# Loading the first K in front of the query weights in a decode step of attention and a gated feed-forward layer

## The chip, the cores and the metric

The kernel runs on one core of a Trainium2 chip. The metric is the device time of one execution in microseconds; lower is better. A core has TensorE for matmuls (PE in the profile; its loads of stationary operands are PEld), VectorE (DVE), ScalarE (ACT), GpSimd (POOL) and SyncE (SP), each with its own instruction stream. They meet through semaphores only. A DMA is issued by one of these streams and carried out by 16 DMA engines that all streams share. On-chip memory is SBUF, with 128 partitions; matmuls write to PSUM.

## What is computed

One token for each of 4 sequences goes through an attention block with a cache and then a gated feed-forward block, each behind a layer norm and with a residual. Cut to what matters:

```python
B, Sq, D = 4, 1, 512
H, Sk, Dh = 32, 8192, 128            # k_cache, v_cache: (B, H, Sk, Dh), bf16

def _A_ref(x, k_cache, v_cache, wq, wo):
    q = (x @ wq).reshape(B, Sq, H, Dh).transpose(0, 2, 1, 3)
    scores = jnp.einsum("bhqd,bhkd->bhqk", q, k_cache) * (Dh ** -0.5)
    p = _softmax(scores, axis=-1)
    o = jnp.einsum("bhqk,bhkd->bhqd", p, v_cache)
    return o.transpose(0, 2, 1, 3).reshape(B, Sq, H * Dh) @ wo

h  = x + _A_ref(_layernorm(x), k_cache, v_cache, wq, wo)
h2 = h + _B_ref(_layernorm(h), w_gate, w_up, w_down)   # (sigmoid(h@w_gate) * (h@w_up)) @ w_down
```

The two caches are 268 MB each, all other inputs together about 13 MB. Every byte is used once.

## The kernel before

The cache is worked through in 32 units (`NU`), each of 4 heads of one sequence. A unit's K is 128 partitions x 64 KB (8.4 MB), and its V likewise. SBUF holds three such places in the tile KV: K of even units in slot 0, K of odd units in slot 1, every V but the last in slot 2. The query weights wq (128 partitions x 32 KB, 4.2 MB) use slot 2 too, ahead of the first V. The names K0, K1, V0 and so on stand for the unit's number below.

At the start, the input x is loaded from ScalarE's queue, normalised and transposed (lines 272 to 292). Then TensorE multiplies it with wq (L301, in two halves of 16 matmuls, waiting for the semaphore of wq), VectorE transposes the result (L308, twice), gathers it in `q_all` (L309), and for each unit lays the query of that unit out as a stationary operand, Lq (`q_window`, L328).

A unit then runs as follows. `scores`: for 16 chunks of K, VectorE transposes a chunk (`k_chunk`, L335) and TensorE multiplies it with the query (four matmuls, L344). There are two places for transposed chunks, so from the third chunk on VectorE waits for TensorE's product with the chunk two before. `maxima`: after the last transpose VectorE writes one word (L361), whose semaphore says that this unit's K is no longer needed; it then finds the maxima (L362 to L367), and ScalarE takes the exponential (L369). In between, `pv` multiplies the weights of the unit before with its V (L405), ScalarE copies the result out (L410), and TensorE gathers it (L415); the first of those gathering matmuls says that this V is no longer needed. `weights` transposes the exponentials (L375). Every stream takes its instructions in the order written, so VectorE comes to L335 of unit 0 only after L308, L309 and L328.

All of the big loads are issued by SP, in one list:

```python
order = [("k", 0)] + [x for u in range(1, NU) for x in (("k", u), ("v", u - 1))] + [("v", NU - 1)]
for n, (x, u) in enumerate(order):
    w = t_qp if n == 2 else None
    if n >= 3:
        w = t_kd[u - 2] if x == "k" else t_kd[NU - 2] if u == NU - 1 else t_vd[u - 1]
```

So wq goes first, then K0 and K1 with no wait, then V0, which waits for the query's matmuls (`t_qp`, since it overwrites wq), then K2, which waits for the transposes of K0 (`t_kd[0]`), V1, which waits for the product with V0 (`t_vd[0]`), K3, which waits for the transposes of K1, and so on in pairs of a V and a K. SP takes them in order: a K whose slot is free still waits behind a V whose slot is not. At the end SP loads wo, w_gate and w_up into slot 1 and w_down into slot 2 (L546 to L557). The final matmuls with w_down (L521), two copies (L529, L530) and the store (L559) follow.

Of the kernel before, what the change touches and what calls it, by code (L numbers as in the profile page):

```python
# [18 lines left out]
class _Prog:  # L19
# [52 lines left out]
    def emit(self, eng, fn, waits=(), incs=1, ch=None):  # L72
        todo = self._waits(eng, waits)
        key = ch or eng
        tok = self.token(key, incs) if incs else None
        self._put(eng, todo, key, fn, incs, 1)
        return tok
# [41 lines left out]
def bass_sequential_preLN__mha_block_cached__glu_gated_glu__decode_kernel(  # L119
# [13 lines left out]
    _, H, S, DH = A_k_cache.shape  # L133
    F = B_w_gate.shape[1]
    assert DH == 128 and H == 32 and D == 512 and F % 128 == 0 and B == 4 and S == 8192
    NC = D // 128
# [17 lines left out]
    prog = _Prog({"p2d": "dve", "d2d": "dve", "a2d": "dve", "d2p": "pe", "a2p": "pe",  # L154
                  "d2a": "act", "p2a": "act",
                  "k0": "dve", "k1": "dve", "v2": "pe"})
    emit = prog.emit

    with ExitStack() as es:
# [40 lines left out]
        def reg(slot, off, size):  # L200
            return KV[:, slot * SLOT + off:slot * SLOT + off + size]
# [26 lines left out]
        t_wq = prog.token("wq", 16)  # L228
# [296 lines left out]
        for t in range(NFT):  # L525
            if t == 0:
# [2 lines left out]
        t_o = [emit("dve", lambda e: e.tensor_copy(o_sb[:, 0:HD], bank[DN][0:B, 0:HD]), [t_d]),  # L529
               emit("act", lambda e: e.activation(o_sb[:, HD:D], bank[DN][32:32 + B, 0:HD], ACT.Copy), [t_d])]  # L530

        prog.dma("sp", "wq", lambda e: e.dma_start(reg(2, 0, NC * H * DH), A_wq.rearrange("(p c) f -> p (c f)", p=128)),
                 tok=t_wq)
        for n, (x, u) in enumerate(order):
            w = t_qp if n == 2 else None
            if n >= 3:
                w = t_kd[u - 2] if x == "k" else t_kd[NU - 2] if u == NU - 1 else t_vd[u - 1]
            slot = slots[x, u]
            cache = A_v_cache if x == "v" else A_k_cache
            src = cache[u // (NU // B), HU * (u % (NU // B)):HU * (u % (NU // B) + 1), :, :].rearrange("h (p r) d -> (h p) (r d)", p=32)  # L540
            prog.dma("sp", f"{x}{slot}", lambda e, src=src, slot=slot: e.dma_start(reg(slot, 0, SLOT), src), [w],  # L541
                     tok=toks[x, u])
        for _ in range(40):
            emit("sp", lambda e: e.nop(), ch="pad")
        k_done, v_done = t_kd[NU - 1], t_vd[NU - 2]
# [46 lines left out]
```

## Time and profile before

| what | value |
|---|---|
| median of 3 runs | 1276.89 us (1276.79 to 1276.95) |
| span of the profiled execution | 1275.6 us |
| PE, DVE, ACT, POOL busy | 779.7, 762.3, 59.0, 5.7 us |
| read from HBM | 550.77 MB |
| transposes of K, L335 | 512, 1232 ns each |
| score matmuls, L344 | 2048, 420 ns each |

The profiled execution's own time is its span and what lies around it, 1.3 us less than the median by the two rows of the table. In the profile a row of an engine's timeline gives the start, the duration, the engine, the line and the operation, then the count if several are merged, and in brackets how long the engine was idle ahead of it and what ended that. "SPq" and "ACTq" are issues of DMAs. In the rows by stretches of time the columns are the length of the stretch, then for PE, PEld, DVE, ACT and POOL the busy time and the number of instructions, then the granted TensorE clock (1.00 is full speed), the summed busy share of the 16 DMA engines and the rate in GB/s.

### The profile page before, as it was taken

How to read it: one execution, taken by the hardware profiler on the slowest of the kernel's cores; microseconds unless marked ns; L12 is line 12 of the kernel's file. 1: busy time of each engine (PE TensorE's matmuls, PEld its weight loads, DVE VectorE, ACT ScalarE, POOL GpSimd, SP SyncE). 2: the span in 40 equal slices, each digit the busy share in tenths (PEclk: the TensorE clock that was granted, in tenths of full speed). 3: DMA queues.
4: the chain of work that ended last, by engine and by line, in shares of the span. 5: the costliest groups of instructions: out<-in, count | busy, mean ns of one | idle time of the engine just before them, and what ended most of it. 6: DMA issues, size and time to landing. Idle time of an engine off the chain costs nothing.

```text
span 1275.6 us, 14073 instructions
## 1 busy us (share of the span) xinstructions
PE 779.7 (61%) x4588; PEld 328.5 (26%) x4636; DVE 762.3 (60%) x917; ACT 59.0 (5%) x114; POOL 5.7 (0%) x22
## 2 busy tenths in 40 slices
PE   1676755557755557655567655567555577555577
PEld 0232222223222223222222222222222232222233
DVE  1876665556665557665567655566655566655571
ACT  2000000000000000000000000000000000000001
POOL 1000000000000000000000000000000000000000
PEclk8888877788877788877788777788777888777888
DMA  9999999999999999999999999999999999999998
GB/s 423 432 426 430 427 450 434 430 430 427 454 430 430 430 427 454 432 427 430 430 452 432 427 430 434 450 430 427 430 440 444 430 427 430 442 442 430 430 427 371
DMA packets 10244, 550.83 MB, mean 432 GB/s; under 512 B 1144, under 2 KB 1152, under 8 KB 1408
## 3 DMA queue, kind: packets, MB, share of 16 engines
q1 hardware_dynamic: 10224, 550.77, 99.7%
q8 instruction: 2, 0.03, 0.0%
q10 hardware_dynamic: 16, 0.01, 0.0%
q14 instruction: 2, 0.02, 0.0%
HBM read 550.77 MB, written 0.00 MB: 432 GB/s over the span
## 4 chain that ended last, share of the span: by engine, by line
DMA 60%; PE 20%; DVE 12%; issue 2%; ACT 1%; SPq 0%; DVEq 0%
DMA KV<-in_A_k_cache_dram 58%; PE PS L344 14%; DVE kT L335 12%; PE PS L405 5%; DMA KV<-in_B_w_down_dram 3%; ACT kT L410 1%; PE PS L415 0%; SPq L541 0%; DVE PTz L375 0%; PE PS L521 0%; DVE KV L529 0%; SPq L557 0%; DVEq L112 0%
## 5 line engine op out<-in xcount | busy, mean ns | idle before, releaser
L344 PE MATMUL PS<-kT,Lq 128*128 128x512 bf16 x2048 | 588.7, 420 | 343.5 <-DVE kT L335 326.4
L335 DVE STREAM_TRANSPOSE kT<-KV 128x1024 f32<-128x1024 f32 x512 | 614.4, 1232 | 300.3 <-DMA KV<-in_A_k_cache_dram 237.5
L344 PEld LDWEIGHTS PS<-kT,Lq 128*128 x2048 | 210.3, 103 | 694.6 <-issue 621.7
L375 DVE STREAM_TRANSPOSE PTz<-E_sb 32x512 bf16<-32x512 bf16 x128 | 89.9, 703 | 129.1 <-PE PS L415 125.5
L405 PE MATMUL PS<-KV,PTz 128*16 128x512 bf16 x2048 | 117.0, 381 | 0.0
L379 PE MATMUL PS<-part,headw 128*128 128x2 f32 x64 | 18.8, 363 | 100.4 <-DVE PTz L375 100.4
L369 ACT ACTIVATE E_sb<-PS,negm 128x512 bf16<-128x512 f32 x32 | 22.0, 687 | 1139.4 <-DVE negm L367 1139.4
L405 PEld LDWEIGHTS PS<-KV,PTz 128*16 128x16 bf16 x2048 | 58.9, 111 | 56.3 <-issue 13.6
L415 PE MATMUL PS<-lane,kT 128*128 128x4 f32 x256 | 33.6, 255 | 31.0 <-ACT kT L410 31.0
L362 DVE TENSOR_REDUCE part<-PS 128x1 f32<-128x512 f32 x32 | 22.1, 691 | 38.7 <-PE PS L344 38.7
L415 PEld LDWEIGHTS PS<-lane,kT 128*128 128x128 f32 x256 | 31.0, 191 | 46.2 <-issue 44.8
L379 PEld LDWEIGHTS PS<-part,headw 128*128 128x128 f32 x64 | 16.0, 310 | 103.7 <-DVE PTz L375 103.7
L410 ACT ACTIVATE kT<-PS,rsb 128x512 f32<-128x512 f32 x32 | 22.0, 687 | 61.5 <-PE PS L405 61.5
L388 PE MATMUL PS<-Lq 128*128 128x512 bf16 x27 | 11.0, 462 | 2.9 <-issue 2.5
L328 DVE TENSOR_TENSOR Lq<-q_all,mask 128x32 bf16<-128x32 bf16 x32 | 9.5, 297 | 0.0
L454 DVE TENSOR_TENSOR kT<-PS,mask 128x512 bf16<-128x512 f32 x1 | 0.7, 692 | 13.3 <-PE PS L415 13.3
L367 DVE STREAM_TRANSPOSE negm<-mxr 128x32 f32<-128x32 f32 x32 | 6.8, 212 | 1.1
L364 DVE STREAM_TRANSPOSE turn<-part 128x32 f32<-128x32 f32 x32 | 6.8, 211 | 1.1
L388 PEld LDWEIGHTS PS<-Lq 128*128 128x128 bf16 x44 | 4.8, 116 | 8.3 <-issue 6.1
L322 PEld LDWEIGHTS PS<-Lq,headw 128*128 128x128 bf16 x32 | 3.5, 108 | 12.8 <-issue 11.3
L396 DVE RECIPROCAL rsb<-PS 128x1 f32<-128x1 f32 x32 | 6.3, 197 | 0.7 <-PE PS L379 0.7
L301 PE MATMUL PS<-KV,kT 128*4 128x512 bf16 x32 | 3.6, 627 | 5.0 <-DMA KV<-in_A_wq_dram 5.0
(70 smaller groups left out, 56.7 us busy)
## 6 DMA issues: line engine op xcount, KB each, us to landing
KV<-in_A_wq_dram SPq DMA_DIRECT2D x1, 4096.0 KB, 12.2
KV<-in_A_wo_dram SPq DMA_DIRECT2D x1, 4096.0 KB, 27.2
KV<-in_B_w_gate_dram SPq DMA_DIRECT2D x1, 1792.0 KB, 31.1
KV<-in_B_w_up_dram SPq DMA_DIRECT2D x1, 1792.0 KB, 34.9
KV<-in_B_w_down_dram SPq DMA_DIRECT2D x1, 1024.0 KB, 32.1
KV<-in_A_k_cache_dram SPq DMA_DIRECT2D x32, 49.6
KV<-in_A_v_cache_dram SPq DMA_DIRECT2D x32, 30.7
KV<-in_B_w_down_dram SPq DMA_DIRECT2D x1, 512.0 KB, 32.9
```

The lines of the kernel that those rows point to most:

```text
L328: t_lq[u] = emit("dve", lambda e, ix: e.tensor_tensor(dst, bass.AP(raw(q_all), at(ix, 0) * (4 * TU) + 4 * (u - TU * t), [[NU * 4, 128], [1 ...
L335: t_tr[u, c] = emit("dve", lambda e: e.transpose(kT[:, (c % 2) * TW:(c % 2 + 1) * TW], KVw[:, o:o + TW]), w, ch="d2p")
L344: ins = e.matmul(bank[SBK], bass.AP(raw(Lq), ix[-1] * 2 + (128 * t + c % 2), [[528, 128], [1, 128]]), rhs, start=False, stop=False, skip_g ...
L362: a = emit("dve", lambda e: e.tensor_reduce(part[:, 0:1], bank[SBK], AX.X, ALU.max), [t_sc[u, NT - 1], t_pool], ch="d2d")
L364: a = emit("dve", lambda e: e.transpose(turn_[:, :], part[:, :]), [a], ch="d2d")
L369: t_exp[u] = emit("act", lambda e: e.activation(E_sb[:, :], bank[SBK], ACT.Exp, bias=negm[:, 0:1], scale=SCALE, accum_out=part[:, 1:2]), [ ...
L375: return [e.transpose(PTz[32 * q:32 * (q + 1), :].rearrange("p (r q c) -> p r q c", r=4, q=4)[:, :, q, :], E_sb[32 * q:32 * (q + 1), :].re ...
L379: t_sum[u] = emit("pe", lambda e: e.matmul(bank[QB[1]][:, 0:2], headw[:, :], part[:, 0:2], start=True, stop=True), [t_ptz[u], t_selc], ch= ...
L388: emit("pe", lambda e: [e.matmul(bank[XS], Lq[:, 0:128], Lq[:, 0:512], start=True, stop=True) for _ in range(n)][-1], [t_ps0, t_lq[NU - 1] ...
L405: made.append(e.matmul(PS[32 * j:32 * j + 16, ob:ob + 512], lhsT, KV[:, slot * SLOT + 512 * k:slot * SLOT + 512 * (k + 1)], start=(k < 4), ...
L410: t_ocp[u] = emit("act", lambda e: e.activation(O_sb, bank[OBK], ACT.Copy, scale=rsb[:, 0:1]), [t_pv[u], t_rs[u]], ch="a2p")
L415: ins = e.matmul(bass.AP(raw(PS), at(ix, 0) * 4 + (512 * EX + 4 * (u - t)), [[4096, 128], [1, 4]]), O_sb[:, 128 * q:128 * (q + 1)], lane[: ...
```

## The change

The load of wq becomes a function, `load_wq`, and is called in the loop behind the first entry of the list. So SP issues K0, wq, K1, and then the rest as before. The waits, the semaphores, the slots and every instruction of the other engines stay as they are; lines behind the edit get a number higher by up to four (the issues of K and V, L541 before, are L543 after).

```diff
-        prog.dma("sp", "wq", lambda e: e.dma_start(reg(2, 0, NC * H * DH), A_wq.rearrange("(p c) f -> p (c f)", p=128)),
-                 tok=t_wq)
+        def load_wq():
+            prog.dma("sp", "wq", lambda e: e.dma_start(reg(2, 0, NC * H * DH), A_wq.rearrange("(p c) f -> p (c f)", p=128)),
+                     tok=t_wq)
+
         for n, (x, u) in enumerate(order):
...
             prog.dma("sp", f"{x}{slot}", lambda e, src=src, slot=slot: e.dma_start(reg(slot, 0, SLOT), src), [w],
                      tok=toks[x, u])
+            if n == 0:
+                load_wq()
```

SP's list at its start, before (the tile KV is named for all of the loads; `s_pe` is the wait of V0 for the query's matmuls, `s_d2x` that of K2 for the transposes of K0, `s_p2x` that of V1 for the product with V0):

```order
L532 DMA KV<-in_A_wq_dram 128x16384 [waits barrier_Pool_Activation_PE_DVE_SP_release]
L541 DMA KV<-in_A_k_cache_dram 128x32768 x2
L541 DMA KV<-in_A_v_cache_dram 128x32768 [waits s_pe]
L541 DMA KV<-in_A_k_cache_dram 128x32768 [waits s_d2x]
L541 DMA KV<-in_A_v_cache_dram 128x32768 [waits s_p2x]
```

The same place of SP's list after the change:

```order
L543 DMA KV<-in_A_k_cache_dram 128x32768 [waits barrier_Pool_Activation_PE_DVE_SP_release]
L533 DMA KV<-in_A_wq_dram 128x16384
L543 DMA KV<-in_A_k_cache_dram 128x32768
L543 DMA KV<-in_A_v_cache_dram 128x32768 [waits s_pe]
L543 DMA KV<-in_A_k_cache_dram 128x32768 [waits s_d2x]
L543 DMA KV<-in_A_v_cache_dram 128x32768 [waits s_p2x]
```

Only the first two entries have changed places. VectorE's list from the query to the end of unit 0's transposes stands after the change as it stood before (`s_k0` is the wait for K0, `s_p2d` that for TensorE's product with an earlier chunk):

```order
L308 STREAM_TRANSPOSE kT<-PS 128x2x8x32 [waits s_pe] x2
L309 CAST q_all<-kT 128x8x4x4 [waits s_dve]
L328 TENSOR_TENSOR Lq<-q_all,mask 128x32 [waits s_pool,s_dve]
L335 STREAM_TRANSPOSE kT<-KV 128x1024 [waits s_k0]
L335 STREAM_TRANSPOSE kT<-KV 128x1024
L335 STREAM_TRANSPOSE kT<-KV 128x1024 [waits s_p2d] x14
L361 MEMSET dumm 128x1
```

Nothing has moved here: the transposes of K0 stand behind the three steps of the query.

## The prediction

> **What bounds the kernel now.** I read the page first: its span, its traffic and the chain that ended last.
>
> ```profile
> span 1275.6 us, 14073 instructions
> ...
> HBM read 550.77 MB, written 0.00 MB: 432 GB/s over the span
> ...
> DMA 60%; PE 20%; DVE 12%; issue 2%; ACT 1%; SPq 0%; DVEq 0%
> ```
>
> The bytes come at one rate from end to end, and no engine is near that. So the question is whether the DMA engines ever run out of queued work. That needs the issues on SP. The waits of SP's queue, then SP's own timeline of the first 120 us (start, duration, issue):
>
> ```profile
> SPq L541 <- PE PS L415: 1122.5, 30, 38.5
> ```
>
> ```profile
> 0.81 0.38 SPq L532 DMA_DIRECT2D KV<-in_A_wq_dram  x1
> 1.24 0.96 SPq L541 DMA_DIRECT2D KV<-in_A_k_cache_dram  x2
> 16.71 0.33 SPq L541 DMA_DIRECT2D KV<-in_A_v_cache_dram  x1
> 53.38 0.33 SPq L541 DMA_DIRECT2D KV<-in_A_k_cache_dram  x1
> 86.88 0.33 SPq L541 DMA_DIRECT2D KV<-in_A_v_cache_dram  x1
> 87.25 1.47 SPq L541 DMA_DIRECT2D KV<-in_A_k_cache_dram  x1
> 119.32 0.33 SPq L541 DMA_DIRECT2D KV<-in_A_v_cache_dram  x1
> ```
>
> In order these are wq, K0 and K1, V0, K2, V1, K3, V2. The reader should see who releases them: V1 and all later V wait for TensorE (L415), which has to finish the product with the V before, so an issue follows the compute. How much is still queued when V1 is issued? The windows of half a microsecond show it. Their last two columns are the summed busy share of the 16 DMA engines and GB/s. A packet is counted whole where it starts: a share of 4.24 in half a microsecond is 4.24 x 0.5 x 16 = 33.9 us of packet time, for 1835 GB/s x 0.5 us = 0.92 MB, 14 packets of 64 KB (a 64 KB row for each partition). So one takes 2.42 us on its engine, and a K or a V is 8 of them on each engine, 19.4 us. The first row is K0's last packets: started by 29.5, ended by 31.9, and K0's landing is seen at 32.27 (below).
>
> ```profile
> 29.00:29.50 0.50, 0.00 (x0) 0.00 (x0) 0.00 (x0) 0.00 (x0) 0.00 (x0) 0.50 4.24 1835
> ```
>
> ```profile
> 89.50:90.00 0.50, 0.00 (x0) 0.00 (x0) 0.47 (x2) 0.00 (x0) 0.00 (x0) 0.50 4.28 1835
> 90.00:90.50 0.50, 0.00 (x0) 0.00 (x0) 0.50 (x1) 0.00 (x0) 0.00 (x0) 0.50 0.00 0
> 90.50:91.00 0.50, 0.41 (x2) 0.41 (x2) 0.03 (x1) 0.00 (x0) 0.00 (x0) 0.50 0.30 131
> 91.00:91.50 0.50, 0.18 (x1) 0.11 (x2) 0.00 (x0) 0.00 (x0) 0.00 (x0) 0.50 0.30 131
> ```
>
> These are the first packets of V1: 14 engines begin it by 90.0, one in 90.5 to 91.0, and the last in 91.0 to 91.5 (I take 91.2). V1 was issued at 86.88, so it was queued in time with a few microseconds to spare, and no more. The tail shows which engine sets the end:
>
> ```profile
> 1271.50:1272.00 0.50, 0.37 (x8) 0.34 (x10) 0.47 (x2) 0.00 (x0) 0.00 (x0) 1.00 0.32 123
> 1272.00:1272.50 0.50, 0.50 (x14) 0.32 (x8) 0.18 (x1) 0.00 (x0) 0.00 (x0) 1.00 0.14 53
> 1272.50:1273.00 0.50, 0.42 (x10) 0.21 (x8) 0.00 (x0) 0.00 (x0) 0.00 (x0) 1.00 0.12 45
> ```
>
> ```profile
> 1273.39 0.09 PEld L521 LDWEIGHTS PS<-KV 128*4 128x4 bf16 x4 [0.33 <-DMA KV<-in_B_w_down_dram]
> ```
>
> Most engines are empty by 1271.5, one or two work on to about 1273, and the last matmuls wait for them. Alone, such an engine is no faster (53 / 16 / 0.14 = 24 GB/s) than in the crowd (1835 / 16 / 4.24 = 27). So the 16 engines are 16 separate servers, and the kernel ends when the latest of them does. What counts is any idle time on that latest engine.
>
> **The change part by part.** K0 now lands about 10 us sooner. That is worth 0: on VectorE the transposes of K0 (L335) stand behind those of the query (L308) and behind L328, as before. The bytes ahead of the later of the two are the same, so wq now lands when K0 did, at about 32.27. The engine rows are, from TensorE and then VectorE:
>
> ```profile
> 13.00 3.59 PE L301 MATMUL PS<-KV,kT 128*4 128x512 bf16 x32 [5.04 <-DMA KV<-in_A_wq_dram]
> ```
>
> ```profile
> 17.77 0.29 DVE L328 TENSOR_TENSOR Lq<-q_all,mask 128x32 bf16<-128x32 bf16 x1
> 32.27 2.37 DVE L335 STREAM_TRANSPOSE kT<-KV 128x1024 f32<-128x1024 f32 x2 [14.21 <-DMA KV<-in_A_k_cache_dram]
> 35.58 1.25 DVE L335 STREAM_TRANSPOSE kT<-KV 128x1024 f32<-128x1024 f32 x1 [0.94 <-PE PS L344]
> 37.29 3.71 DVE L335 STREAM_TRANSPOSE kT<-KV 128x1024 f32<-128x1024 f32 x3 [0.46 <-PE PS L344]
> ```
>
> From wq's landing to the end of L328 it takes 17.77 + 0.29 - 13.00 = 5.06 us. Before, that lay under K0's transfer (VectorE idles 14.21 us ahead of L335). Now it stands between the landing and the first transpose, so the scores of unit 0 start at about 32.27 + 5.1 = 37.4, **5.1 us later**.
>
> Who feels it? V0, which waits for the query's matmuls, is issued at 16.71 + 19.3 = 36.0. The engines are then on K1 until 31.9 + 19.4 = 51.3: cost 0, 15 us of cover. K2, which waits for the transposes of K0, goes from 53.38 to about 58.5. V0 keeps the engines until 70.7: cost 0, 12 us of cover. Then V1:
>
> ```profile
> 59.75 2.37 DVE L335 STREAM_TRANSPOSE kT<-KV 128x1024 f32<-128x1024 f32 x2
> ```
>
> ```profile
> 91.74 2.37 DVE L335 STREAM_TRANSPOSE kT<-KV 128x1024 f32<-128x1024 f32 x2 [1.21 <-DMA KV<-in_A_k_cache_dram]
> 95.05 1.25 DVE L335 STREAM_TRANSPOSE kT<-KV 128x1024 f32<-128x1024 f32 x1 [0.94 <-PE PS L344]
> 96.76 1.25 DVE L335 STREAM_TRANSPOSE kT<-KV 128x1024 f32<-128x1024 f32 x1 [0.46 <-PE PS L344]
> 98.47 2.37 DVE L335 STREAM_TRANSPOSE kT<-KV 128x1024 f32<-128x1024 f32 x2 [0.46 <-PE PS L344]
> ```
>
> Unit 1 starts at 59.75 with no wait for a DMA, K1 having landed long before. So from 32.27 to V1's issue at 86.88 all is compute, and a late start is handed on in full: 86.88 + 5.1 = 92.0.
>
> One term is uncertain, the TensorE clock. At a unit's start VectorE idles for TensorE while its clock is low: 0.94 + 0.46 = 1.40 us in unit 0 and 0.94 + 0.46 + 0.46 = 1.86 in unit 2. The clock in the rows above is 0.50 at 29.0 and again at 90. If the query's matmuls, now just ahead of the scores, leave the clock up, unit 0 loses none of its 1.40; if both units come out like unit 2, each loses about 0.5 more. That makes V1's issue 90.6 to 93.0. Between the query's matmuls and the first scores lie some 2.8 us with almost no matmul, so I don't expect the gain, and a usual unit falls between 1.40 and 1.86: I take 92.2. [...]
>
> The last piece is how long after an issue the packets flow. The trace shows that with empty engines once, at the start, where wq was issued at 0.81:
>
> ```profile
> 1.50:2.00 0.50, 0.00 (x0) 0.00 (x0) 0.00 (x0) 0.50 (x1) 0.43 (x3) 1.00 1.60 401
> 2.00:2.50 0.50, 0.07 (x1) 0.07 (x1) 0.09 (x1) 0.50 (x1) 0.50 (x2) 1.00 1.95 590
> 2.50:3.00 0.50, 0.50 (x1) 0.00 (x1) 0.50 (x1) 0.49 (x2) 0.24 (x2) 1.00 0.16 66
> ...
> 3.50:4.00 0.50, 0.00 (x0) 0.00 (x0) 0.00 (x0) 0.50 (x2) 0.31 (x2) 1.00 1.52 655
> 4.00:4.50 0.50, 0.00 (x0) 0.00 (x0) 0.00 (x0) 0.50 (x2) 0.41 (x3) 1.00 0.91 393
> ```
>
> Its 32 KB packets start 6, 9 and 1 in the first three windows: 0.7 to 2.2 us after the issue, most by 1.3. They are slow, however. The second packets start around 3.9, and with 1.21 us for one (half of 2.42) the first are worth a start at 2.7, 1.9 us after the issue. I take 1.7, nearer to that, and keep 0.7 and 2.2 as ends.
>
> **Sum.** V1's packets flow at 92.2 + 1.7 = 93.9 on all engines. The latest engine would have begun at 91.2. It loses 93.9 - 91.2 = **2.7 us**; the others lose some 4, of which their lead of 1.5 hides a part, and end no later. K3 is issued right behind V1, with no wait of its own. V2 went at 119.32; unit 2 starts at 90.53 + 5.3 = 95.8 instead of 91.74, so V2 goes at about 123.4 and flows by 125.1, while K3 keeps even the early engines until 89.7 + 2 x 19.4 = 128.5 without the stall: cost 0. From then on the lost time is only carried to the end. The span becomes 1275.6 + 2.7 = 1278.3. The median of the runs, 1276.89, lies 1.3 above the profiled span, so 1276.9 + 2.7 = **1279.6 us, 0.21% more**. About 0.2% (2.55 us) is what a measurement of this kernel can tell from no change, and the forecast sits on that line. With the ends of its terms the loss is 90.6 + 0.7 - 91.2 = 0.1 to 93.0 + 2.2 - 91.2 = 4.0.
>
> **The rivals.**
> - *Hidden by the late engine, not slower.* The delay falls into the lead that V1 has. It decides at an issue of V1 by 91.2 less the start time: if the clock stays up through the query (issue at 90.6) and packets flow after 0.7 to 1.3, the loss is 0.1 to 0.7, giving 1277.0 to 1277.6. For it: 15 of 16 first packets did start within 1.7 us. Against it: those packets were slow, and the gap of 2.8 us on TensorE.
> - *A quick first byte.* The start after an issue is short because the queue is already running. With the same 92.2 and the lower end, 0.7, the loss is 1.7: 1278.6. [...]
> - *The lag goes, faster.* The late engine's 1.5 us arise between the even packets at 29 and the uneven ones at 90. If the stall lines the engines up and V1 is on time, up to 1.5 us come back: 1275.4. It needs V1 to be issued by about 88, so a delay of 1.1 instead of 5.1; nothing shows such cover.
> - *A second stall.* If V2 is late too (a slower unit 2, another half microsecond of clock, slow first packets), 1 to 2 us are added: 1281 to 1282. Its cover of 3.4 us speaks against it.
> - *No change of order.* If the engines mix wq and K0, both land near 32.3 and the same delay follows; this isn't a separate case.
>
> **How the numbers follow.** The forecast, a stall of 1.9 to 4.0 us at V1: 0.74, of which a bit over two thirds lies above 2.55. The hidden delay: 0.10. The quick first byte: 0.10. The lag that goes: 0.03. A second stall: 0.03. Slower by over 0.2% is 0.50 + 0.03 = 0.53; faster by over 0.2% gets 0.02; the rest, 0.45, is the same. The range leaves out the lowest of the hidden cases and the second stall: 1277.5 to 1280.9, the upper end being 1276.9 + 4.0.
>
> **What would show it.** In the profile after: K0's packets first; L301 at about 32.3; L335 at 37.4 behind L328 and not behind a DMA; V1's issue near 92.2 (90.6 to 93.0); in half-microsecond windows no packet starts from about 90 to 93, then all 16 together; every later K landing (91.74 aside) 2 to 3 us later, up to the end. The runs should spread more than now. It is wrong if V1's issue stays below 90, if the gap in the packets is missing, or if the end doesn't move with K3's landing.

## The result and the profile after

The kernel after took 1280.53 us (median of 7 runs, 1280.38 to 1281.84), the kernel before 1276.79 us (7 runs, 1276.56 to 1276.95). The ratio is 1.0031 with a 95% interval of 1.0022 to 1.004: slower by about 3.7 us, clear of noise. The execution that was profiled is the one of 1281.84, so it lies at the upper end; a second profile, of an execution of 1279.87, comes with the last experiment.

```profile
span 1280.6 us, 14121 instructions
```

SP's timeline of the kernel after (start, duration, issue) answers to the seven rows of before:

```profile
0.81 0.38 SPq L543 DMA_DIRECT2D KV<-in_A_k_cache_dram  x1
1.24 0.42 SPq L533 DMA_DIRECT2D KV<-in_A_wq_dram  x1
1.71 0.61 SPq L543 DMA_DIRECT2D KV<-in_A_k_cache_dram  x1
35.97 0.33 SPq L543 DMA_DIRECT2D KV<-in_A_v_cache_dram  x1
58.61 0.33 SPq L543 DMA_DIRECT2D KV<-in_A_k_cache_dram  x1
92.38 0.33 SPq L543 DMA_DIRECT2D KV<-in_A_v_cache_dram  x1
92.75 0.43 SPq L543 DMA_DIRECT2D KV<-in_A_k_cache_dram  x1
123.29 0.33 SPq L543 DMA_DIRECT2D KV<-in_A_v_cache_dram  x1
```

V0, K2 and V1 go 19.3, 5.2 and 5.5 us later than before, V2 4.0. The start of the compute, from TensorE's and VectorE's timelines of the kernel after:

```profile
32.26 3.58 PE L301 MATMUL PS<-KV,kT 128*4 128x512 bf16 x32 [24.29 <-DMA KV<-in_A_wq_dram]
```

```profile
37.02 0.29 DVE L328 TENSOR_TENSOR Lq<-q_all,mask 128x32 bf16<-128x32 bf16 x1
37.13 2.36 DVE L335 STREAM_TRANSPOSE kT<-KV 128x1024 f32<-128x1024 f32 x2
40.44 1.25 DVE L335 STREAM_TRANSPOSE kT<-KV 128x1024 f32<-128x1024 f32 x1 [0.94 <-PE PS L344]
42.15 1.25 DVE L335 STREAM_TRANSPOSE kT<-KV 128x1024 f32<-128x1024 f32 x1 [0.46 <-PE PS L344]
43.86 1.25 DVE L335 STREAM_TRANSPOSE kT<-KV 128x1024 f32<-128x1024 f32 x1 [0.46 <-PE PS L344]
```

The first transpose no longer waits for a DMA: K0 is there, and it stands behind the query. The DMA engines around V1's issue, in half microseconds, kernel after (the last two columns are the engines' summed share and GB/s; a packet is counted where it starts):

```profile
90.00:90.50 0.50, 0.50 (x16) 0.30 (x12) 0.00 (x0) 0.00 (x0) 0.00 (x0) 1.00 0.00 0
90.50:91.00 0.50, 0.50 (x12) 0.01 (x4) 0.00 (x0) 0.00 (x0) 0.00 (x0) 1.00 0.00 0
91.00:91.50 0.50, 0.00 (x1) 0.00 (x0) 0.00 (x0) 0.37 (x1) 0.00 (x0) 1.00 0.00 0
...
93.00:93.50 0.50, 0.02 (x1) 0.00 (x0) 0.36 (x1) 0.00 (x0) 0.00 (x0) 1.00 3.99 1311
93.50:94.00 0.50, 0.00 (x0) 0.00 (x0) 0.47 (x2) 0.00 (x0) 0.00 (x0) 1.00 2.27 786
...
96.00:96.50 0.50, 0.40 (x2) 0.41 (x2) 0.47 (x2) 0.00 (x0) 0.00 (x0) 0.50 0.30 131
96.50:97.00 0.50, 0.18 (x1) 0.10 (x2) 0.50 (x1) 0.00 (x0) 0.00 (x0) 0.50 4.54 1966
```

No packet starts in the first three rows, where before 14 + 1 + 1 engines went on from K2 to V1 between 89.5 and 91.5. Then 10 and 6 packets start in one microsecond, slowly (3.99 of share for 1311 GB/s is 3.2 us for a packet of 64 KB), and the second packets follow at about 96.5. Less 2.42 us, the flow is as if begun at 94.1, 1.7 us after the issue.

How the loss goes on, by the landings of K3, of K11 and of the last K. Before, then after:

```profile
130.35 2.37 DVE L335 STREAM_TRANSPOSE kT<-KV 128x1024 f32<-128x1024 f32 x2 [7.37 <-DMA KV<-in_A_k_cache_dram]
439.37 2.37 DVE L335 STREAM_TRANSPOSE kT<-KV 128x1024 f32<-128x1024 f32 x2 [7.80 <-DMA KV<-in_A_k_cache_dram]
1212.12 2.37 DVE L335 STREAM_TRANSPOSE kT<-KV 128x1024 f32<-128x1024 f32 x2 [7.42 <-DMA KV<-in_A_k_cache_dram]
```

```profile
133.41 2.37 DVE L335 STREAM_TRANSPOSE kT<-KV 128x1024 f32<-128x1024 f32 x2 [6.46 <-DMA KV<-in_A_k_cache_dram]
443.18 2.37 DVE L335 STREAM_TRANSPOSE kT<-KV 128x1024 f32<-128x1024 f32 x2 [7.91 <-DMA KV<-in_A_k_cache_dram]
1216.28 2.37 DVE L335 STREAM_TRANSPOSE kT<-KV 128x1024 f32<-128x1024 f32 x2 [7.72 <-DMA KV<-in_A_k_cache_dram]
```

The shift is 3.06 us at K3, 3.81 at K11, 4.16 at the last K, and 5.0 at the end of the span. A landing goes by the latest engine: in the kernel before 14 engines begin V2, which follows K3, between 128.0 and 129.0 and the last one between 129.5 and 130.0, and K3's landing is seen at 130.35. So about 3 us are seen on that engine at once, and some 2 more by the end. The end of the traffic in the kernel after:

```profile
1276.00:1276.50 0.50, 0.00 (x0) 0.00 (x0) 0.47 (x3) 0.00 (x0) 0.00 (x0) 1.00 0.96 373
1276.50:1277.00 0.50, 0.39 (x8) 0.36 (x10) 0.27 (x1) 0.00 (x0) 0.00 (x0) 1.00 0.21 78
1277.00:1277.50 0.50, 0.50 (x12) 0.30 (x8) 0.00 (x0) 0.00 (x0) 0.00 (x0) 1.00 0.06 25
1277.50:1278.00 0.50, 0.42 (x10) 0.23 (x8) 0.00 (x0) 0.00 (x0) 0.00 (x0) 1.00 0.06 25
```

The early engines are empty at about 1276.5 instead of 1271.5, 5.0 us later, and here too work goes on for 1.5 us behind them. The last rows also say on how many engines: a share of 0.12 is 0.12 x 16 = 1.9 engines in the kernel before, 0.06 is 1.0 in the kernel after.

### The profile page after: what moved, and what is told of

Read it like the earlier page. It is cut to its first block, busy times and chain, and to the rows that moved or that the text cites. A ratio compares the mean times of both kernels' runs of the same rounds, so it can differ in the third digit from the quotient of the medians.

```text
span 1280.6 us, 14121 instructions
## 1 busy us (share of the span) xinstructions
PE 801.9 (63%) x4636; PEld 329.1 (26%) x4636; DVE 761.9 (59%) x917; ACT 59.0 (5%) x114; POOL 5.7 (0%) x22
## 5 line engine op out<-in xcount | busy, mean ns | idle before, releaser
L322 PE MATMUL PS<-Lq,headw 128*128 128x512 bf16 x32 | 18.8, 586 | 10.9 <-issue 9.5
L388 PE MATMUL PS<-Lq 128*128 128x512 bf16 x44 | 13.7, 480 | 0.2 <-issue 0.2
```

Source lines behind the costliest of these rows:

```text
L322: emit("pe", lambda e: e.matmul(bank[bk], headb, zeros, start=True, stop=False, skip_group_check=True), waits, incs=0)
L388: emit("pe", lambda e: [e.matmul(bank[XS], Lq[:, 0:128], Lq[:, 0:512], start=True, stop=True) for _ in range(n)][-1], [t_ps0, t_lq[NU - 1] ...
```

## The experiments

Two questions: does the late issue of V1 make the whole loss, or does the order of the loads cost something by itself; and from which issue on does it cost? For the second there are two theories: the late engine (only what goes beyond 91.2, when the latest engine would take up V1, is lost) and all engines (all that goes beyond 89.7, when the early ones would).

**A shorter unit 0, order as after.** The scores of unit 0 leave out the last 4 of its 16 chunks.

```diff
-            for c in range(NT):
+            n = NT if u else NT - 4
+            for c in range(n):
...
+            if u == 0:
+                t_sc[0, NT - 2], t_sc[0, NT - 1] = t_sc[0, n - 2], t_sc[0, n - 1]
```

> The kernel after, with the last 4 of the 16 chunks of unit 0 left out (4 transposes and 16 score matmuls), so unit 0's scores are those of 12 chunks only. Loads and their order are those of the kernel after. Theory (V1 is issued too late): V1's issue moves from 92.4 by 4 x 1.24 us to about 87.4, its packets flow at about 89.2, ahead of the latest engine's 91.2, and the time falls back to 1276.8 (1276.4 to 1277.3). Rival (the order of the first loads costs by itself, by larger first packets or by where wq stands): 1280.5, as after.

Measured: 1277.13 us (11 runs), ratio to before 1.0001 (0.9992 to 1.001); V1 was issued at 86.14, 1.3 us sooner than expected. The order of the loads costs nothing if V1 is in time; the rival falls.

**A late unit 0, order as before.** VectorE transposes one chunk of K0 four times more, ahead of unit 0.

```diff
+            for _ in range(0 if u else 4):
+                t_late[u] = emit("dve", lambda e: e.transpose(kT[:, 0:TW], KVw[:, (NT - 1) * TW:NT * TW]), [toks["k", u], t_late.get(u)], ch="d2d")
             for c in range(NT):
```

> The kernel before, wq first, with 4 needless transposes of the last chunk of K0 put ahead of unit 0's own on VectorE, about 1.3 us each. Theory: V1's issue moves from 86.9 to about 92.1, packets flow 1.75 us later at 93.9, the latest engine loses 2.6 to 2.9 us, and with the 0.6 that the typical execution of the kernel after shows beyond that, the time is 1279.4 to 1280.6. Rival (order of the loads): 1276.8.

Measured: 1281.23 us (5 runs), ratio 1.0036 (1.0023 to 1.005). V1's issue, with wq first as before:

```profile
92.40 0.33 SPq L545 DMA_DIRECT2D KV<-in_A_v_cache_dram  x1
```

It stands where it stands in the kernel after, and the span, 1280.5 us, is that kernel's within 0.1. So the late issue is enough. The median lies 0.6 us above the upper end that was expected.

**Half of that delay.** The same edit with 2 in place of 4.

> The kernel before with 2 needless transposes instead of 4. Theory (nothing is lost until V1's packets flow later than the latest engine's 91.2): V1's issue at about 89.5, flow at 91.2, a loss of 0 to 0.5 us: 1276.8 to 1277.4. Rival (a late start is handed to the end in proportion): half of what 4 transposes cost, about 1278.5.

Measured: 1279.09 us (11 runs, 1277.77 to 1280.62), ratio 1.0017 (1.0008 to 1.0026). V1 was issued at 89.58, as expected, but the loss is not 0 to 0.5 us, it is 2.2: the threshold was put too late. K3 landed only 0.33 us later than before and the span was 2.0 us longer, so here too most of the loss shows itself after K3 (whose landing goes by the latest engine). This gave the second theory, all engines.

**The clock kept up.** In the kernel after, TensorE works on zeros while it waits for wq, and between the query and the scores.

```diff
+        emit("pe", lambda e: e.matmul(bank[XS], PTz[:, 0:128], PTz[:, 0:512], start=True, stop=True), [t_pool, t_xn], incs=0)
+        warm(4, 22, [])      # a loop of 22 turns with 4 such matmuls
         t_qr = []
...
+        warm(2, 5, [])
         emit("pe", lambda e: e.matmul(bank[EX][:, 0:128], PTz[:, 0:128], PTz[:, 0:128], start=True, stop=False,
```

> The kernel after with matmuls on zeros (into a PSUM bank that is free then) while TensorE waits for wq, and ten more between the query's matmuls and the first scores, so that the clock is up for both. Theory: the query's matmuls take 1.8 us instead of 3.6, VectorE's first idle times in unit 0 (0.94 + 0.46 + 0.46 us) go, V1's issue moves from 92.4 to about 88.8 and flows at 90.5: no loss, 1276.8 (1276.4 to 1277.5). Rival (the start after the query isn't what makes V1 late): 1280.5.

Measured: 1279.63 us (11 runs, 1278.55 to 1281.52), ratio 1.0023 (1.0014 to 1.0032). Unit 0 did lose its waits, but the matmuls ended 2.9 us ahead of wq and the query's matmuls took 3.42 us, hardly less than 3.58. So V1 went at 90.89, not at 88.8, and a loss remained. In this profile the clock was down at the very end (0.50 from about 1275), and the last matmuls took 3.15 us instead of 2.15:

```profile
1275.31 3.15 PE L533 MATMUL PS<-KV 128*4 128x256 bf16 x28 [1.08 <-DMA KV<-in_B_w_down_dram]
```

That is 1.0 us which is not the stall's. Inconclusive by itself; the run with the clock kept up in both units, below, answers it.

**A quarter of the delay.** One transpose in place of four.

> The kernel before with 1 needless transpose ahead of unit 0's own. Two theories of where the loss begins. Late engine (the latest engine's 91.2 decides): V1's issue at 88.2 to 88.6, flow at 90.0 to 90.4, no loss: 1276.9. All engines (from the 89.7 of the early engines on, every microsecond counts, since some engine falls behind again later, and 0.65 us come on top in units 3 to 9 once the engines have been emptied together): 0.3 to 0.7 us of stall and up to 0.65 on top: 1277.2 to 1278.2.

Measured: 1277.78 us (11 runs, 1276.68 to 1281.12), ratio 1.0011 (1.0002 to 1.002); V1 at 88.42, span 1276.4. For all engines, against the late engine. One of the 11 executions took 1281.12, longer than the median of the kernel after; no profile of it was taken, and its cause stays open.

**Twice the delay.** Eight transposes.

> The kernel before with 8 needless transposes, about 10.2 us. V1's issue at about 97.2, flow at 98.9. Late engine: 98.9 - 91.2 = 7.7, with 0.6 as in the first runs 8.3: 1285.2. All engines: 98.9 - 89.7 = 9.2, with 0.65 on top 9.9: 1286.8.

Measured: 1287.65 us (5 runs), ratio 1.0082 (1.0068 to 1.0096); V1 at 98.22, a microsecond later than expected: VectorE waited 0.94 + 0.46 + 0.46 us for TensorE in unit 0 and in unit 1, against 0.94 + 0.46 and 0.94 + 0.38 in the kernel before. With that issue the late engine would give 1286.2 and all engines 1287.8. The profiled execution is the longest of the five, 1288.6, with a span of 1287.3; its last matmuls took 3.15 us here too, and without that 1.0 us it would be 1287.6. For all engines again.

**The clock kept up in both units.** As above with 24 turns instead of 22, and TensorE busy between units 0 and 1.

```diff
+                emit("pe", lambda e: e.matmul(bank[XS][:, 0:128], headb, bass.AP(raw(q_all), 0, [[NU * 4, 128], [1, 128]]),
+                                              start=True, stop=True), [t_q, t_selc], incs=0)
...      # and a loop of 10 turns with 8 such matmuls
```

> As the run with the clock up, but the matmuls on zeros go on until wq is due, and TensorE is kept busy between units 0 and 1 too (80 small matmuls into a free PSUM bank). Theory: the query's matmuls take 1.8 us, neither unit 0 nor unit 1 waits for a slow TensorE at its start; V1's issue moves from 92.4 by 1.8 + 1.9 + 1.6 to about 87.1, in time on any engine: 1276.9 (1276.5 to 1277.5). Rival (the clock is worth no more than the first such run showed): 1279.6.

Measured: 1277.24 us (11 runs, 1276.92 to 1279.18), ratio 1.0003 (0.9994 to 1.0012). From TensorE's timeline of this kernel, the query's matmuls, and from SP's, V1's issue:

```profile
32.27 1.90 PE L312 MATMUL PS<-KV,kT 128*4 128x512 bf16 x32 [1.12 <-DMA KV<-in_A_wq_dram]
```

```profile
87.37 0.33 SPq L565 DMA_DIRECT2D KV<-in_A_v_cache_dram  x1
```

With wq behind K0, full computation and V1 in time, the loss is gone. It does not beat the kernel before: where V1 is in time there is nothing left to win on this path.

**The kernel after again**, unchanged.

> The kernel after, once more, beside the others on the same chip, for the spread of its runs and a second profile: 1280.5 (1280.3 to 1281.9). All engines: V1's flow less 89.7, and 0.65 on top, should give its profile's span less 1275.6. Late engine: V1's flow less 91.2, and 0.6.

Measured: 1280.76 us (6 runs, 1279.87 to 1281.99), ratio 1.0032 (1.002 to 1.0044). The profiled execution is the fastest of them, with a span of 1278.6 us. Its unit 0, and its issue of V1:

```profile
37.35 11.11 DVE L335 STREAM_TRANSPOSE kT<-KV 128x1024 f32<-128x1024 f32 x9
```

```profile
90.33 0.33 SPq L543 DMA_DIRECT2D KV<-in_A_v_cache_dram  x1
```

Nine transposes follow each other with no wait for TensorE, where the first profile of the same kernel waits 0.94 + 0.46 + 0.46 us. V1 goes 2.05 us sooner, and the span is 2.0 us shorter, which is as much as the spread of the runs (2.1 us). From this issue all engines gives a span 90.33 + 1.7 - 89.7 + 0.65 = 3.0 us longer than before, and the late engine 1.4; it is 3.0.

**All profiles together.** The third column is the span less the 1275.6 us of before, the fourth V1's issue less 87.4.

| kernel | V1's issue | span longer by | issue - 87.4 |
|---|---|---|---|
| shorter unit 0 | 86.14 | 0.2 | in time |
| before | 86.88 | 0 | in time |
| clock up, both units | 87.37 | 0.3 | 0.0 |
| late by 1 | 88.42 | 0.8 | 1.0 |
| late by 2 | 89.58 | 2.0 | 2.2 |
| after, second profile | 90.33 | 3.0 | 2.9 |
| clock up | 90.89 | 4.7, with 1.0 from the last matmuls | 3.5 |
| after | 92.38 | 5.0 | 5.0 |
| late by 4 | 92.40 | 4.9 | 5.0 |
| late by 8 | 98.22 | 11.7, with 1.0 from the last matmuls | 10.8 |

One line holds for both orders: nothing is lost up to an issue at about 87.4, and from there every microsecond counts in full, to within 0.3 us. The 87.4 was read off the table, and agrees with the early engines' 89.7 less 1.7 us to flow less 0.65 us of later loss, 87.35.

## Why the prediction was right, point by point

The change did what it was read to do. K0's early landing was worth nothing; wq landed at 32.26 (32.27 forecast), unit 0 began at 37.13 (37.4), V0 and K2 were covered, V1 went at 92.38 in the first profile (92.2) and at 90.33 in the second (90.6 to 93.0, so 0.3 below the range), V2 at 123.29 (123.4) with no second stall. The flow began 1.7 us after the issue (1.7). K3 landed 3.06 us later (2.7), and the last K 4.16, where 2 to 3 was forecast up to the end. Direction and mechanism were right, and 1280.53 lies in the range; the forecast of 2.7 us was 1.0 us too small. Two terms were off, in opposite directions. That the median stayed in the range is in part luck: with the forecast issue of 92.2 the line of the table gives 1276.9 + 4.8 = 1281.7, above the range, and 2 of the 7 executions (1281.57 and 1281.84) were above it.

The step that failed is the sum over the engines: "the others lose some 4, of which their lead of 1.5 hides a part, and end no later. ... From then on the lost time is only carried to the end." The late engine's lag is no fixed reserve. In the first profile the early engines lost 94.1 - 89.7 = 4.4 us, and ended 5.0 us later; the stall had made all engines even, and at the end one was 1.5 us behind again, as before.

What puts an engine behind can be read in finer windows. Beside the kernel's own loads both pages list queues that load instructions, one of them with two packets:

```profile
q8 instruction: 2, 0.03, 0.0%
```

Before, around the first of them, then at the second; after, at the first:

```profile
87.43:87.44 0.01, 0.01 (x1) 0.00 (x0) 0.00 (x0) 0.00 (x0) 0.00 (x0) 1.00 5.76 1638
88.33:88.35 0.02, 0.00 (x0) 0.00 (x0) 0.00 (x0) 0.00 (x0) 0.00 (x0) 0.50 9.14 3277
1257.51:1257.52 0.01, 0.00 (x0) 0.00 (x0) 0.01 (x1) 0.01 (x1) 0.00 (x0) 1.00 6.04 1638
```

```profile
89.70:89.71 0.01, 0.01 (x6) 0.00 (x0) 0.00 (x0) 0.00 (x0) 0.00 (x0) 1.00 7.91 1639
```

Each row holds one packet. 1638 GB/s in 0.01 us are 16 KB, half of the 0.03 MB of that queue, and 5.76 x 0.01 x 16 = 0.92 us. In the kernel before this packet runs from 87.43 to 88.35, a 64 KB packet of K2 starts as it ends and takes 9.14 x 0.02 x 16 = 2.92 us instead of 2.42, and that gives 91.26, where the latest engine takes up V1. The lag of 1.4 us is thus an instruction load among the data. In the kernel after, the first one falls at 89.70, as the engines run dry, and the stall evens out what it leaves. The second comes at 1257.5 before and at 1261.3 after (in all ten traces 18 to 21 us ahead of the end of the span), so in both kernels one engine falls behind late, whatever happened at V1. In between, one round of packets, before and then after:

```profile
1190.50:1191.00 0.50, 0.50 (x4) 0.10 (x1) 0.50 (x1) 0.00 (x0) 0.00 (x0) 1.00 2.12 918
1191.00:1191.50 0.50, 0.23 (x2) 0.08 (x1) 0.50 (x2) 0.00 (x0) 0.00 (x0) 1.00 2.12 918
1191.50:1192.00 0.50, 0.50 (x3) 0.30 (x4) 0.50 (x1) 0.00 (x0) 0.00 (x0) 1.00 0.30 131
1192.00:1192.50 0.50, 0.47 (x3) 0.00 (x0) 0.43 (x1) 0.00 (x0) 0.00 (x0) 1.00 0.30 131
```

```profile
1191.00:1191.50 0.50, 0.41 (x2) 0.01 (x1) 0.41 (x2) 0.00 (x0) 0.00 (x0) 1.00 4.84 2097
```

Before, the engines still start 7, 7, 1 and 1; after, all 16 in one half microsecond. So the old lag did go with the stall and stayed away, but the second instruction load made a new one of the same size before the end. That is why the end follows the early engines, and why two engines are late at the end before and one after. This is read from the traces; no run moved an instruction load.

Of the rest, 0.75 us came between K3 and K11 (3.06 to 3.81). It shows in every profile whose V1 was issued after 89, 0.45 to 0.8 us, and hardly where V1 was in time (0.15 with the shorter unit 0, 0.26 with the clock up in both units). In the first profile it is packets that take 2.5 us instead of 2.42: those that start from 104 to 460 us take 0.6 us more in sum on each engine than in the kernel before. What makes these packets longer no run shows.

The term that was too large is V1's issue. By the line of the table the median of 1280.53, 3.7 us above before, belongs to an issue near 91.1, not 92.2; the execution with the median time was not profiled, so this is an estimate. The step reads "I don't expect the gain" from the query's matmuls leaving the clock up; the second profile shows that gain in full, with no wait for TensorE in unit 0. The corrected sum can be checked on the two profiles: 2.7 + 0.2 for the issue of 92.38 + 1.5 for the lead + 0.65 for the later loss is 5.05 (measured 5.0), and with 1.9 less for the issue of 90.33 it is 2.95 (measured 3.0).

Of the rivals, the hidden delay and the quick first byte fall with the table and with the windows: the packets that start 0.6 to 1.6 us after the issue are slow (3.2 and 3.0 us for 64 KB, by the two rows, instead of 2.42), and the flow is that of a start after 1.7. V1's first packets start between 93.3 and 93.4, 0.9 to 1.0 us after its issue; counted from there, the loss would be taken 0.7 to 0.8 us too small. In the start of the kernel before, the prediction reads "most by 1.3" of the first packets, but its rows show 6 of 16 by 1.2 us after the issue and 15 by 1.7; the 1.7 that it went on with doesn't need that reading. The second stall did not come: in the kernel after VectorE waits 6.46 us for K3. The lag that goes: it did go, and another came at 1261.

The spread was forecast, and the two profiles of the kernel after show where it comes from. TensorE's first score matmuls of unit 0, first profile, then second:

```profile
38.52 6.25 PE L344 MATMUL PS<-kT,Lq 128*128 128x512 bf16 x16 [0.54 <-DVE kT L335]
```

```profile
38.73 2.16 PE L344 MATMUL PS<-kT,Lq 128*128 128x512 bf16 x8 [0.76 <-DVE kT L335]
```

One takes 391 ns in the first and 270 ns in the second. In the kernel before, 12 of them take 4.46 us, for most of which the clock column reads 0.50, and 8 take 2.17 us where it reads 1.00. By these times the first profile's unit 0 starts at the low clock and the second's at the full one; the column doesn't show it, it reads 1.00 for both from 32 to 42 us. VectorE waited 1.86 us for TensorE in unit 0 of one and not at all in that of the other, and V1's issue moved by 2.05. What decides at which clock a unit starts no run shows. In the kernel before the waits differ from unit to unit as well (1.40 us in unit 0, 1.32 in unit 1, 1.86 in unit 2), but its V1 has 0.5 us to spare, and its 7 runs lie within 0.4 us.

## What to carry to other kernels

When transfers are the bound, judge a change in the order of loads by the first issue that it can make late, not by the load that it makes early: here K0 came sooner for nothing, and 5 us more compute ahead of V1, whose reserve was half a microsecond, were lost almost one for one. Take the reserve from the engines that run dry first, and count the time from an issue to full flow (1.7 us here). A lead of some DMA engines over the latest one was no reserve here, since another engine fell behind by as much just ahead of the end.

## What the runs showed that was not expected

- After an idle moment the first packets of 64 KB took about 3.2 us instead of 2.42 (share 3.99 for 1311 GB/s), so the time to full flow, 1.7 us, was longer than that to the first packet, 0.9 to 1.0 us.
- A DMA engine left alone was no faster than in the crowd (24 to 27 GB/s), so in the kernel before a lag of 1.4 us stayed from 91 to 1192 us.
- In the kernel before two packets of 16 KB that load instructions (0.92 and 0.97 us) each set one DMA engine behind by about 1.4 us, with a slower data packet behind them (2.92 us instead of 2.42, and 1.69 us for 32 KB instead of 1.21), and the last loads ended 1.5 us later on about two engines (shares of 0.14 and 0.12) than on most of the others.
- The same last 28 matmuls took 2.13 to 2.17 us in eight of the ten profiles and 3.15 us in two (clock up, late by 8), where the clock fell to 0.50 at that moment. That is 1 us on the end whatever the change.
